# The first transform stage of the later batches: row fold on GpSimd, column fold on VectorE, products in four 64x64 tiles

## The chip, the core and the metric

The kernel runs on one core of one Trainium2 chip. A core has five engines that run their own queues and meet through semaphores: TensorE (PE; its weight loads are shown apart as PEld), VectorE (DVE), ScalarE (ACT), GpSimd (POOL) and SyncE (SP, which here only issues DMAs). The metric is the device time of one execution in microseconds, as the median of several runs. Before the change it is 1962.98 us, the median of three runs (1962.75 to 1963.18).

## What is computed

The reference takes eight batches of 3008 positions by 256 features, all in float32. It applies a Fourier transform along both axes, keeps the real part, and sends it through a two-layer network whose activation is h times cos(h):

```python
X = np.fft.fft(np.fft.fft(x, axis=1), axis=2).real   # x: (8, 3008, 256)
h = X.reshape(24064, 256) @ w_in                     # w_in: (256, 2048)
out = (h * np.cos(h)) @ w_out                        # w_out: (2048, 256)
```

## The kernel before

**The transform.** The 3008 positions are written as 47 rows (s2) by 64 columns (s1). The transform along the positions is therefore done in two stages: first over the 47 rows, for each of the 64 columns, and then over the columns. The input is real, so column i is handled together with column 64 - i: there are 32 pairs, `NI`, numbered i. The transform along the features folds feature d with feature 256 - d, so that 128 numbers are left of each 256, once as a sum (e = 0) and once as a difference (e = 1); the cosines and sines that this needs are multiplied into the network's first weights at the start.

*First stage, in chunks of four pairs (c = 0 to 7).* `load_x` (L151) brings 16 pairs into one of two buffers `xs[p]`, with the 47 rows of column i and the 47 rows of column 64 - i on 110 partitions. `fold` (L237) adds and subtracts features d and 256 - d of a chunk, 110 partitions by 4x127 (508) elements, once for each e; for the first batch VectorE does it, for the later ones GpSimd. `first_half` (L271) then makes two products for each chunk, one for each e, with 110 rows, 64 output columns and 512 moving columns (L286). They write the lower and the upper 64 partitions of one PSUM bank, `pz`. Chunk 0 has its pair 0 apart (L283), and chunks 0 and 4 also compute feature 128 for 16 pairs (`middle`, L253, product at L256). ScalarE copies `pz` to `zs` (L291) with feature 128 beside it (L292), and `store_z` (L298) sends `zs` to DRAM.

*Second stage.* `load_z` reads this back in another order; `second_half` (L321) makes 4 products of 128 columns for each of six groups (L328, bank `pb`), and ScalarE copies them to `pq`. `pz` and `pb` take turns in the one bank with the tag "fft".

**The network.** A batch has six groups of output columns, and a group has eight steps, each with 256 of the 2048 hidden units, so there are 384 steps (48 a batch). Step t has `mm1` (L484: four products into a bank `H`, two with `WC` and two with `WS`), then on ScalarE `act_e` (`ew`, L495), `seed` for the next step's `H` (L454), `act_sin` (L525) and two `act_round` (L515), and on VectorE `dve_h` (L500), `dve_frac` (L519), `dve_g` (L529) and `dve_s` (L540, L550), and at last `mm2` (L574), seven products of 256 columns that are summed over the eight steps in four banks `M`. The second half of the fourth of these banks is not used by `mm2`. The seven products are the fast form of a 2x2 block product: their inputs `S` are sums that VectorE makes. The stages of one step are spread over four turns of the main loop (`LAG` = 3). At the end of a group ScalarE reads the `M` banks (`take_m`, L595), GpSimd adds them up (L626), VectorE transposes (`store_out`, L670) and SP stores.

**What sets the order.** The order is written out by hand in the main loop (L756); every engine runs its queue in that order. The transform of batch b lies beside the network of batch b - 1: `transform` (L364) puts its calls into lists by step number, counted here from the first step of batch b - 1. Calls of `todo` (loads, `first_half`, stores, second half) are issued at the end of a step; calls of `aside` are GpSimd's, and `beside` (L747) ties each of them to the step's last `dve_s` (L550), so that GpSimd starts together with VectorE's reads of PSUM. Before the change a chunk folds in steps o and o + 1, makes its products at the end of step o + 2 and is stored in step o + 3, with o = 7 + 8*(c//2) + 2*(c%2); `load_z` is in step 37, and the six second halves are in steps 41, 43, 45, 49, 52 and 55.

Of the kernel before, what the change touches and what calls it, by code (L numbers as in the profile page):

```python
# [18 lines left out]
ND = 256  # L19
# [16 lines left out]
    return STEP * (r % 16) + 3 * side + r // 16  # L36


def _consts():

    s2 = np.arange(N2)
    j = np.arange(NJ)
    th = 2.0 * np.pi * np.outer(s2, j) / N2
    thm = 2.0 * np.pi * np.outer(46 - s2, j) / N2
    thh = 2.0 * np.pi * np.outer(s2 + 0.5, j) / N2
    z = np.zeros((N2, NJ))
    pad = np.zeros((2 * N2, 16))

    def stack(a, b, c, d):
        m = np.block([[a, b], [c, d]]).reshape(2 * N2, 2, NJ)
        near, far = m[:, :, 0:JA], m[:, :, JA:]
        return np.concatenate(
            [near.reshape(2 * N2, 2 * JA), far.reshape(2 * N2, 2 * (NJ - JA)), pad], axis=1
        )

    LE = stack(np.cos(th), -np.sin(th), np.cos(thm), -np.sin(thm))
    LO = stack(np.sin(th), np.cos(th), -np.sin(thm), -np.cos(thm))
    LE0 = stack(np.cos(th), z, z, np.cos(thh))  # L60
    LO0 = stack(np.sin(th), z, z, np.sin(thh))
    L = np.concatenate([LE, LO, LE0, LO0], axis=1)
    rows = np.zeros((128, 256))
    for side in range(2):
        for r in range(N2):
            rows[_place(side, r)] = L[N2 * side + r]
    L = rows

    k2 = np.arange(64)
    i = np.arange(NI)  # L70
    B = np.zeros((128, NJ, 128))
    for jj in range(NJ):
        phi = 2.0 * np.pi * np.outer(i, 47 * k2 + jj) / SEQ
        blk = np.concatenate([np.cos(phi), np.sin(phi)], axis=0)
        blk[0] = 1.0
        blk[NI] = np.where(k2 % 2 == 0, 1.0, -1.0)
        blk = blk.reshape(2, 2, 16, 64)
        for half in range(2):
            for r in range(2):
                for e in range(2):  # L80
                    p = 64 * half + 32 * e + r
                    B[p : p + 31 : 2, jj, 64 * e : 64 * e + 64] = blk[r, half]

    c = np.arange(ND)
    d = np.arange(128)
    ang = 2.0 * np.pi * np.outer(c, d) / ND
    CS = np.concatenate([np.cos(ang), -np.sin(ang)], axis=1) / TWO_PI
    CS[:, 128] = np.where(c % 2 == 0, 1.0, -1.0) / TWO_PI
    return (
        L.astype(np.float32),  # L90
        B.reshape(128, NJ * 128).astype(np.float32),
        CS.astype(np.float32),
    )
# [28 lines left out]
def kernel(  # L122
# [8 lines left out]
    NB = x.shape[0]  # L131
    L_np, B_np, CS_np = _consts()
    LCS_dr = nc.inline_tensor(
        np.concatenate([L_np, CS_np[0:128], CS_np[128:256]], axis=1), name="dft_L"
    )
    ident_dr = nc.inline_tensor(np.eye(128, dtype=np.float32), name="ident")
    B_dr = nc.inline_tensor(B_np, name="dft_B")

# [9 lines left out]

    xs = [spool.tile([128, XP * ND], FP, tag=f"xp{p}", name="xp") for p in range(2)]

    def load_x(b, p):  # L151
        xv = xs[p][0 : 16 * STEP].rearrange("(e g) c -> e g c", g=STEP)
        i0 = XP * p
        back = nc.sync if b or p else nc.scalar

        def load(queue, g, c0, c1, cols, **more):
            for m in range(3):
                k = 15 if m == 2 else 16
                queue.dma_start(
                    out=xv[0:k, g + m, ND * c0 : ND * c1].rearrange("e (i d) -> e i d", d=ND),  # L160
                    in_=x_r[b, 16 * m : 16 * m + k, cols],
                    **more,
                )

        load(nc.sync, 0, 0, XP, slice(i0, i0 + XP), max_dma_last_dim=2048)
        c0 = 0 if p else 1
        load(back, 3, c0, XP, slice(64 - i0 - c0, 64 - i0 - XP, -1))
        if p == 0:
            load(nc.sync if b else nc.gpsimd, 3, 0, 1, slice(32, 33))

    LCS = cpool.tile([128, 768], FP, tag="LCS", name="LCS")
    L = LCS[:, 0:256]
# [14 lines left out]
    def load_bj(c0, c1):  # L187
        nc.sync.dma_start(out=BJ[:, c0:c1], in_=B_dr.ap()[:, c0:c1])

    def load_ident():  # L190
        nc.sync.dma_start(out=ident, in_=ident_dr.ap())

# [10 lines left out]
    mid = cpool.tile([128, NI], FP, tag="mid", name="mid")  # L203
    nc.sync.dma_start(out=LCS, in_=LCS_dr.ap())
    load_w(0)
    nc.vector.memset(xs[0][0:XR, 0:2048], 0.0)  # L206
    nc.gpsimd.memset(xs[0][0:XR, 2048:4096], 0.0)
    nc.vector.memset(VX[:, 0:512], 1.0)
    nc.vector.memset(ones, 1.0)
    nc.vector.memset(mask, 1.0)  # L210
    nc.vector.memset(mask[0:1], 0.0)
    nc.vector.memset(xs[1][0:XR], 0.0)
    load_x(0, 0)
    for xf in xf0:
        nc.gpsimd.memset(xf[64:128], 0.0)
# [4 lines left out]
    WC = cpool.tile([128, NDFF], FP, tag="WC", name="WC")  # L220
    WS = cpool.tile([128, NDFF], FP, tag="WS", name="WS")
    wn = cpool.tile([128, 16], FP, tag="wn", name="wn")
    nrow = cpool.tile([1, NDFF], FP, tag="nrow", name="nrow")
    xf1 = [cpool.tile([128, 2 * IP * 128], FP, tag=f"xf{i}", name="xf") for i in range(2)]
    for xf in xf1:
        nc.gpsimd.memset(xf[0:XR, 512:1024:128], 0.0)

    bank = {"fft": 1, "M": 4, "H": 3}

# [1 line left out]
        return ppool.tile([128, 512], FP, tag=tag, bufs=bank[tag], name=name)  # L231


    def folded(b, c):
        return (xf1 if b else xf0)[c % 2]

    def fold(b, c, e):  # L237
        lo = IP * (c % 4)
        xv = xs[c // 4].rearrange("r (i d) -> r i d", d=ND)[0:XR, lo : lo + IP]
        fv = folded(b, c).rearrange("r (e i d) -> r e i d", e=2, d=128)[0:XR]  # L240
        if e == 0:
            (nc.scalar.copy if b else nc.gpsimd.tensor_copy)(  # L242
                out=fv[:, 0, :, 0], in_=xv[:, :, 0]
            )
        return (nc.gpsimd if b else nc.vector).tensor_tensor(  # L245
            out=fv[:, e, :, 1:128],
            in0=xv[:, :, 1:128],
            in1=xv[:, :, 255:128:-1],
            op=ALU.subtract if e else ALU.add,
        )  # L250

    def middle(b, p):
        xm = xs[p].rearrange("r (i d) -> r i d", d=ND)[0:XR, :, 128]  # L253
        pm = acc[live[0]][3][64:128, 256 : 256 + XP] if b else psum("pm", "M")[64:128, 0:XP]
        for i0, i1, q in ((0, 1, 2), (1, XP, 0)) if p == 0 else ((0, XP, 0),):
            nc.tensor.matmul(  # L256
                pm[:, i0:i1],
                lhsT=L[0:XR, 64 * q : 64 * q + 64],
                rhs=xm[:, i0:i1],
                start=b == 0,  # L260
                stop=True,
                skip_group_check=b > 0,
            )
        nc.scalar.copy(out=mid[64:128, XP * p : XP * p + XP], in_=pm)

    acc = {}
    started = {}
# [2 lines left out]

    def first_half(b, c):  # L271

        if c % 4 == 0:
            middle(b, c // 4)
        rows = XR if b else 128
        fv = folded(b, c).rearrange("r (e c) -> r e c", e=2)[0:rows]
        LE, LO, LE0, LO0 = (L[0:rows, 64 * q : 64 * q + 64] for q in range(4))
        pz = psum("pz", "fft" if b else "M")
        a = 128 if c == 0 else 0
        for e, (w, w0) in enumerate(((LE, LE0), (LO, LO0))):  # L280
            rows = slice(64 * e, 64 * e + 64)
# [4 lines left out]
            nc.tensor.matmul(  # L286
                pz[rows, a:512], lhsT=w, rhs=fv[:, e, a:512], start=True, stop=True
            )
        tag, n = ("zs", 4) if b or c < 4 else ("pq", 8)
        zs = spool.tile([128, 512], FP, tag=tag, bufs=n, name="zs")  # L290
        nc.scalar.copy(out=zs, in_=pz)  # L291
        nc.scalar.copy(out=zs[64:128, 0:512:128], in_=mid[64:128, IP * c : IP * c + IP])  # L292
# [5 lines left out]
    def store_z(b, c, far):  # L298
# [4 lines left out]
        zd = zds[b, far].rearrange("(h e i r) (j d) -> h i (r j) e d", h=2, e=2, r=2, d=128)  # L303
        zs = zss[b, c].rearrange("(e y) (i d) -> y e i d", e=2, d=128)
        y0 = 2 * JA if far else 0
        for e in range(2):
            queue = nc.scalar if b == 0 and not far and (e or c > 3) else nc.sync
            queue.dma_start(
                out=zd[half, IP * q : IP * q + IP, :, e].rearrange("i y d -> y i d"),
                in_=zs[y0 : y0 + 2 * n, e],  # L310
# [49 lines left out]

    todo = {}
    aside = {}

    def transform(b):  # L364
        t0 = (b - 1) * NG * 8
# [1 line left out]
        def at(o, *call):  # L367
            todo.setdefault(t0 + o, []).append(call)

        at(3, load_x, b, 0)  # L370
        at(14, load_x, b, 1)
        for c in range(NCH):
            o = 7 + 8 * (c // 2) + 2 * (c % 2)
            aside.setdefault(t0 + o, []).append((fold, b, c, 0))
            aside.setdefault(t0 + o + 1, []).append((fold, b, c, 1))
            at(o + 2, first_half, b, c)
            at(o + 3, store_z, b, c, 0)
            at(o + 3, store_z, b, c, 1)
        at(37, load_z, b, 0)
        at(37, load_z, b, 1)  # L380
        for g, o in enumerate((41, 43, 45, 49, 52, 55)):
            at(o, second_half, b, g)

    def fold_weights(e, n, tag="M"):
# [11 lines left out]
        if e:  # L396
            nc.scalar.activation(
                out=W[:, cols], in_=pw, func=AF.Copy, bias=0.0, scale=mask[:, 0:1]
            )
            nc.vector.tensor_copy(out=nrow[:, cols], in_=pw[0:1, :])  # L400
        else:
            nc.scalar.copy(out=W[:, cols], in_=pw)

# [1 line left out]

    def send_wn(n):
        wds[n] = dpool.tile([1, 512], FP, tag="wd", bufs=4, name="wd")
        nc.sync.dma_start(out=wds[n], in_=nrow[:, 512 * n : 512 * n + 512])

    def take_wn(n):  # L410
        nc.sync.dma_start(
# [54 lines left out]
    def seed_first(s):  # L466
        T = s.T
        s.pq, s.nb = ready[s.b, s.grp]
        for u in range(2):
            nc.tensor.matmul(  # L470
                s.H[:, u * T : u * T + T],
                lhsT=nrow[:, 128 * u : 128 * u + 128],
                rhs=s.pq[0:1, T : 2 * T],
                start=False,
                stop=True,
# [249 lines left out]
    for c in range(NCH // 2):  # L725
# [4 lines left out]
    opening = {  # L730
        0: ((combine_w2, 6, 8), (take_wn, 2)) + tuple((store_z, 0, c, 1) for c in (4, 5)),
        1: ((send_wn, 3),) + tuple((store_z, 0, c, 1) for c in (6, 7)) + ((take_wn, 3),),
        2: ((load_z, 0, 1), (load_bj, 1024, NJ * 128)),
        5: ((second_half, 0, 1),),
        10: ((second_half, 0, 2), (load_ident,)),
        14: ((second_half, 0, 3),),
        18: ((second_half, 0, 4),),
        22: ((second_half, 0, 5),),
    }
    per = NG * 8  # L740
    n = len(steps)

    def step(t, last=None):
        s = steps[t] if 0 <= t < n else None
# [11 lines left out]
    for t in range(n + LAG + 1):  # L756
        cur, prev, old, done = step(t), step(t - 1), step(t - 2), step(t - LAG)
        if cur:
            if t % per == 0 and cur.b + 1 < NB:
                transform(cur.b + 1)  # L760
            mm1(cur, 0)
            act_e(cur)
            if t == 0:
# [22 lines left out]
            act_sin(prev)  # L786
        if old:
            dve_s(old, 0)
        if done:
            dve_s(done, 2)  # L790
        ahead = dve_s(old, 1) if old else None
# [50 lines left out]
```

## Time and profile before

| What | Value |
|---|---|
| median of 3 runs | 1962.98 us (1962.75 to 1963.18) |
| the profiled execution, and its span | 1964.43 us, 1962.7 us |
| granted TensorE clock, mean | 0.995 |
| VectorE busy | 1747.2 us (89%) |
| ScalarE busy | 1521.2 us (78%) |
| GpSimd busy | 377.7 us (19%) |
| DMA | 88.67 MB, mean 45 GB/s |

A float32 product shows as two MATMUL records and two LDWEIGHTS records, so 9216 MATMUL records are 4608 products. "Busy" counts overlapping records once. A line of the timeline is the start in us, how long the merged records last, the engine, the line of the kernel, the operation, output<-inputs, the shape and how many records; in square brackets stands the idle time before it and who ended it. L12 is line 12 of the kernel before.

### The profile page before, as it was taken

Reading aid. Unit: us, or ns where it says so; the run is one execution under the profiler, and the core shown is the slowest. Engines: PE = TensorE matmul, PEld = TensorE weight load, DVE = VectorE, ACT = ScalarE, POOL = GpSimd, SP = SyncE. Lnnn points to the kernel's source line nnn. Section 1 sums busy time; section 2 is a strip of 40 time slices with the busy share of each in tenths; the row PEclk is TensorE's granted clock in tenths of the full one; section 3 lists DMA queues with packets and bytes.
Section 4 is the critical chain, followed back from the end, with each engine's and each line's share of the span. In section 5 each row is a group of like instructions: output and inputs, shape, how many; then the busy total and the mean of one; then the engine's idle time right before and its main releaser. Section 6 shows DMA issues by size and latency. Waiting matters only on the chain.

```text
span 1962.7 us, 29008 instructions
## 1 busy us (share of the span) xinstructions
PE 1940.6 (99%) x9216; PEld 1689.6 (86%) x9216; DVE 1747.2 (89%) x3217; ACT 1521.2 (78%) x2762; POOL 377.7 (19%) x432
## 2 busy tenths in 40 slices
PE   7999999999999999999999999999999999999998
PEld 3888899888998889988898888988889888898887
DVE  4888998899889998899889988998899898999998
ACT  2877778777787788777877787778877887778775
POOL 2122202222022211222112221122211222111100
PEclk8999999999999999999999999999999999999999
DMA  6320112202111112120121201211012201110010
GB/s 198 90 67 22 57 25 55 54 22 60 29 50 50 29 54 53 25 57 23 54 54 27 56 24 53 53 50 35 24 49 60 56 22 56 22 28 10 12 23 22
DMA packets 159960, 88.67 MB, mean 45 GB/s; under 512 B 104845, under 2 KB 150204, under 8 KB 158656
## 3 DMA queue, kind: packets, MB, share of 16 engines
q1 hardware_dynamic: 158320, 85.72, 16.7%
q8 instruction: 73, 1.20, 0.3%
q10 hardware_dynamic: 1392, 1.05, 0.2%
q14 instruction: 79, 0.65, 0.1%
q0 software_dynamic: 96, 0.05, 0.0%
HBM read 49.51 MB, written 37.28 MB: 44 GB/s over the span
## 4 chain that ended last, share of the span: by engine, by line
PE 97%; DMA 1%; DVE 1%; ACT 0%; issue 0%; ACTq 0%; POOL 0%; DVEq 0%; POOLq 0%; SPq 0%
PE M L574 58%; PE H L484 34%; PE pz L286 3%; PE pb L328 2%; DMA xp<-in_x_dram 1%; DMA zd<-zs 0%; PE pw L388 0%; DMA z<-zd 0%; PE M L256 0%; DVE r L519 0%; PE pz L283 0%; PE H L470 0%; DVE xp L206 0%; POOL xf L242 0%; DVE ob L670 0%
## 5 line engine op out<-in xcount | busy, mean ns | idle before, releaser
L574 PE MATMUL M<-S,VX 128*128 128x256 f32 (+1 forms) x2304 | 612.8, 375 | 0.0
L574 PEld LDWEIGHTS M<-S,VX 128*128 128x128 f32 x2304 | 438.8, 191 | 48.9
L515 ACT ACTIVATE r<-H 128x512 f32<-128x512 f32 (+1 forms) x384 | 226.0, 589 | 252.9 <-DVE h L500 252.9
L525 ACT ACTIVATE r<-r 128x1024 f32<-128x1024 f32 (+1 forms) x384 | 395.2, 1029 | 24.4 <-DVE r L519 18.2
L500 DVE TENSOR_TENSOR h<-ew,H 128x512 f32<-128x512 f32 (+1 forms) x384 | 259.3, 675 | 165.6 <-PE H L484 90.6
L484 PE MATMUL H<-pq,WC 128*128 128x256 f32 (+1 forms) x1536 | 395.2, 380 | 1.1 <-ACT H L454 1.1
L484 PE MATMUL H<-pq,WS 128*128 128x256 f32 (+1 forms) x1536 | 388.8, 376 | 0.6 <-ACT ew L495 0.5
L574 PE MATMUL M<-r,w 128*128 128x256 f32 (+1 forms) x1536 | 388.0, 375 | 0.0
L454 ACT ACTIVATE H<-nb,wn 128x256 f32<-128x256 f32 (+1 forms) x766 | 362.2, 473 | 13.9
L484 PEld LDWEIGHTS H<-pq,WC 128*128 128x128 f32 x1536 | 284.5, 191 | 73.9 <-ACT r L515 23.5
L574 PEld LDWEIGHTS M<-r,w 128*128 128x128 f32 x1536 | 300.8, 197 | 26.7
L484 PEld LDWEIGHTS H<-pq,WS 128*128 128x128 f32 x1536 | 292.8, 191 | 35.7 <-ACT ew L495 2.0
L495 ACT ACTIVATE ew<-H 128x512 f32<-128x512 f32 (+1 forms) x384 | 225.9, 588 | 73.4 <-PE H L484 68.1
L519 DVE SCALAR_TENSOR_TENSOR r<-r,H 128x512 f32<-128x512 f32 (+1 forms) x384 | 258.8, 674 | 20.4 <-ACT r L515 1.6
L626 POOL TENSOR_TENSOR cb<-cb,mr 128x256 f32<-128x256 f32 (+3 forms) x188 | 157.9, 850 | 541.4 <-DVE S L550 344.5
L540 DVE TENSOR_TENSOR S<-r 128x512 f32<-128x512 f32 (+1 forms) x384 | 259.1, 675 | 0.1
L519 DVE SCALAR_TENSOR_TENSOR r<-r,h 128x512 f32<-128x512 f32 (+1 forms) x384 | 258.6, 673 | 0.0
L529 DVE SCALAR_TENSOR_TENSOR r<-h,r 128x512 f32<-128x512 f32 (+1 forms) x384 | 258.2, 672 | 0.0
L529 DVE SCALAR_TENSOR_TENSOR r<-H,r 128x512 f32<-128x512 f32 (+1 forms) x384 | 256.0, 667 | 0.9 <-ACT r L525 0.5
L515 ACT ACTIVATE r<-h 128x512 f32<-128x512 f32 (+1 forms) x384 | 236.0, 614 | 0.0
L574 PE MATMUL M<-S,w 128*128 128x256 f32 (+1 forms) x768 | 225.7, 375 | 1.0 <-DVE S L550 1.0
L245 POOL TENSOR_TENSOR xf<-xp 110x508 f32<-110x508 f32 x112 | 141.7, 1265 | 436.1 <-DVE S L550 281.6
(75 smaller groups left out, 1449.9 us busy)
## 6 DMA issues: line engine op xcount, KB each, us to landing
out_dram<-ob SPq DMA_DIRECT2D x728, 32.0 KB
xp<-in_x_dram SPq DMA_DIRECT2D x48, 256.0 KB
zd<-zs SPq DMA_DIRECT2D x128, 80.0 KB
z<-zd SPq DMA_DIRECT2D x8, 1280.0 KB
xp<-in_x_dram SPq DMA_DIRECT2D x38, 240.0 KB
nb<-nd SPq DMA_DIRECT2D x40, 128.0 KB
wr<-in_moe_w_in_dram SPq DMA_DIRECT2D x4, 512.0 KB
w<-in_moe_w_out_dram SPq DMA_DIRECT2D x2, 1024.0 KB
```

Of the source, the lines that this page charges most:

```text
L245: return (nc.gpsimd if b else nc.vector).tensor_tensor(out=fv[:, e, :, 1:128], in0=xv[:, :, 1:128], in1=xv[:, :, 255:128:-1], op=ALU.subtr ...
L454: nc.scalar.activation(out=s.H[:, u * T : u * T + T], in_=s.nb[:, 0:T], func=AF.Copy, bias=0.25, scale=wn[:, f : f + 1],)
L484: nc.tensor.matmul(s.H[:, u * T : u * T + T], lhsT=W[:, 128 * f : 128 * f + 128], rhs=s.pq[:, e * T : e * T + T], start=False, stop=True, ...
L495: nc.scalar.mul(out=s.ew[:, 0 : 2 * s.T], in_=s.H[:, 0 : 2 * s.T], mul=2.0)
L500: nc.vector.tensor_tensor(out=s.h[:, 0 : 2 * T].rearrange("p (u t) -> p u t", u=2)[:, :, ::-1], in0=s.ew[:, 0 : 2 * T].rearrange("p (u t) ...
L515: nc.scalar.activation(out=r, in_=h, func=AF.Copy, bias=BIG, scale=1.0)
L519: nc.vector.scalar_tensor_tensor(out=r, in0=r, scalar=-BIG, in1=h, op0=ALU.add, op1=ALU.subtract)
L525: nc.scalar.activation(out=r, in_=r, func=AF.Sin, bias=0.0, scale=SIN_SCALE)
L529: nc.vector.scalar_tensor_tensor(out=r, in0=h, scalar=-0.25, in1=r, op0=ALU.add, op1=ALU.mult)
L540: return nc.vector.tensor_tensor(out=sv[:, 0:2], in0=gv[:, 2:3].to_broadcast([128, 2, T]), in1=gv[:, 0:4:3], op=ALU.subtract,)
L574: nc.tensor.matmul(acc[key][m // 2][:, 256 * (m % 2) : 256 * (m % 2) + T], lhsT=w, rhs=a, start=first, stop=s.fp == 7, skip_group_check=True,)
L626: return nc.gpsimd.tensor_tensor(out=o, in0=a, in1=b, op=ALU.subtract if less else ALU.add)
```

## The change

Only batches 1 to 7 are changed; batch 0 keeps its way. Three things are different.

- **The row fold comes first.** `load_later_x` puts the two columns of a pair on the same partitions (row s of one beside row S - s of the other), 16 of the 32 pairs on partitions 0 to 48 and the other 16 on 64 to 112 ("sets"). A load is made in four calls of seven DMAs, and the two unpaired columns (0 and 32) have four DMAs of their own (`load_ends`). GpSimd's call in `aside` is now `fold_rows`: 113 partitions by 512 elements, once for each e, in place of the fold over features. VectorE has a new list, `between`, issued in the middle of a step: `fold_cols`, which folds the features of what GpSimd left, 113 by 2x127 (254) elements, and once a batch the unpaired columns, 113 by 127. ScalarE copies feature 0.
- **The products are 64x64 tiles.** A chunk has four products (`first_half_later`): for each e and each set, with 49 rows, 64 output columns and 256 moving columns. Set 0 writes `pz`, set 1 writes the unused half of the fourth `M` bank, which ScalarE sets to zero a step earlier (`clear_spare`). ScalarE copies two pieces of 128x256 in place of one of 128x512. Feature 128 takes four products of 7 or 8 columns for 16 pairs (`middle_later`); with chunk 0 there are a fifth one of 1 column and two of 128 columns for the unpaired columns.
- **The order moves.** Batches 2 to 7 load x in steps -20 to -17 and -9 to -6, that is 28 and 39 steps into the network of batch b - 2; batch 1 loads in steps 2 to 5 and 13 to 16. The products of odd chunks, and their stores, come one step later; `load_z` is in step 38, and the first three second halves in 42, 44 and 46. A chunk is stored by eight DMAs in place of four.

```diff
+    def load_later_x(b, p, s, set_):
+        i0 = 16 * set_ + 8 * p
+        skip = 1 if s and i0 == 0 else 0
+        cols = slice(64 - i0 - skip, 56 - i0, -1) if s else slice(i0, i0 + 8)
+        to = xs[p].rearrange("r (s i d) -> r s i d", s=2, d=ND)[:, s, skip:8]
+        for k in range(7):
...
+            nc.sync.dma_start(out=to[part], in_=x_r[b, rows, cols])
...
+    def clear_later():
+        nc.gpsimd.memset(xz, 0.0)
+        for xf in xf1:
+            nc.gpsimd.memset(xf[:, 256:512:128], 0.0)
+        nc.gpsimd.memset(xfz[:, 128:129], 0.0)
...
+    def fold_rows(b, c, e):
+        lo = 2 * (c % 4) * ND
+        xv = xs[c // 4].rearrange("r (s c) -> r s c", s=2)[0:XL, :, lo : lo + 2 * ND]
+        return nc.gpsimd.tensor_tensor(
+            out=xs2[e][0:XL],
+            in0=xv[:, 0],
+            in1=xv[:, 1],
+            op=ALU.subtract if e else ALU.add,
+        )
+
+    def fold_cols(to, src, e):
+        fv = to.rearrange("r (e i d) -> r e i d", e=2, d=128)[0:XL, e]
+        xv = src.rearrange("r (i d) -> r i d", d=ND)[0:XL]
+        nc.vector.tensor_tensor(
+            out=fv[:, :, 1:128],
+            in0=xv[:, :, 1:128],
+            in1=xv[:, :, 255:128:-1],
+            op=ALU.subtract if e else ALU.add,
+        )
+        if e == 0:
+            nc.scalar.copy(out=fv[:, :, 0], in_=xv[:, :, 0])
...
+    def middle_later(pz, p):
+        pm = pz[64:128, 256:272]
+        for set_ in range(2):
+            i0 = 1 if set_ == p == 0 else 0
+            for s in range(2):
+                xm = xs[p].rearrange("r (s i d) -> r s i d", s=2, d=ND)[0:XL, s, i0:8, 128]
+                nc.tensor.matmul(
+                    pm[:, 8 * set_ + i0 : 8 * set_ + 8],
+                    lhsT=weights(2 + set_, 0, XL),
+                    rhs=xm,
+                    start=s == 0,
+                    stop=s == 1,
+                )
+        if p == 0:
+            nc.tensor.matmul(
+                pm[:, 0:1], lhsT=weights(4, 0, XL), rhs=xz[0:XL, 128:129], start=True, stop=True
+            )
...
+    def clear_spare():
+        nc.scalar.activation(
+            out=acc[live[0]][3][:, 256:512],
+            in_=VX[:, 0:256],
+            func=AF.Copy,
+            bias=0.0,
+            scale=0.0,
+        )
+
+    def first_half_later(b, c):
+        pz = psum("pz")
+        spare = acc[live[0]][3][:, 256:512]
+        if c % 4 == 0:
+            middle_later(pz, c // 4)
+        if c == 0:
+            for e in range(2):
+                nc.tensor.matmul(
+                    pz[64 * e : 64 * e + 64, 0:128],
+                    lhsT=weights(4 + e, 0, XL),
+                    rhs=xfz[0:XL, 128 * e : 128 * e + 128],
+                    start=True,
+                    stop=True,
+                )
+        xf = xf1[c % 2]
+        for e in range(2):
+            for set_ in range(2):
+                r0, r1 = 64 * set_, 64 * set_ + XT
+                c0 = 128 if set_ == c == 0 else 0
+                nc.tensor.matmul(
+                    (spare if set_ else pz)[64 * e : 64 * e + 64, c0:256],
+                    lhsT=weights(e, r0, r1),
+                    rhs=xf[r0:r1, 256 * e + c0 : 256 * e + 256],
+                    start=set_ == 0,
+                    stop=True,
+                    skip_group_check=set_ == 1,
+                )
+        zs = spool.tile([128, 512], FP, tag="zs", bufs=4, name="zs")
+        nc.scalar.copy(out=zs[:, 256:512], in_=spare)
+        nc.scalar.copy(out=zs[:, 0:256], in_=pz[:, 0:256])
...
+        zss[b, c] = zs
...
+        if b:
+            for e in range(2):
+                for h in range(2):
+                    nc.sync.dma_start(
+                        out=zd[h, 2 * c : 2 * c + 2, :, e].rearrange("i y d -> y i d"),
+                        in_=zs[y0 : y0 + 2 * n, e, 2 * h : 2 * h + 2],
+                    )
+            return
...
-        at(3, load_x, b, 0)
-        at(14, load_x, b, 1)
+        for p, o in enumerate((2, 13) if b == 1 else (-20, -9)):
+            for k in range(4):
+                at(o + k, load_later_x, b, p, k % 2, k // 2)
+        at(4 if b == 1 else -16, load_ends, b)
         for c in range(NCH):
             o = 7 + 8 * (c // 2) + 2 * (c % 2)
-            aside.setdefault(t0 + o, []).append((fold, b, c, 0))
-            aside.setdefault(t0 + o + 1, []).append((fold, b, c, 1))
-            at(o + 2, first_half, b, c)
-            at(o + 3, store_z, b, c, 0)
-            at(o + 3, store_z, b, c, 1)
-        at(37, load_z, b, 0)
-        at(37, load_z, b, 1)
-        for g, o in enumerate((41, 43, 45, 49, 52, 55)):
+            f = o + 2 + c % 2
+            for e in range(2):
+                aside.setdefault(t0 + o + e, []).append((fold_rows, b, c, e))
+                between.setdefault(t0 + o + e + 1, []).append(
+                    (fold_cols, xf1[c % 2], xs2[e], e)
+                )
+            at(f - 1, clear_spare)
+            at(f, first_half, b, c)
+            at(f + 1, store_z, b, c, 0)
+            at(f + 1, store_z, b, c, 1)
+        for e in range(2):
+            between.setdefault(t0 + 7 + e, []).append((fold_cols, xfz, xz, e))
+        at(38, load_z, b, 0)
+        at(38, load_z, b, 1)
+        for g, o in enumerate((42, 44, 46, 49, 52, 55)):
             at(o, second_half, b, g)
...
         if old:
             dve_s(old, 0)
+        for call in between.pop(t, ()):
+            call[0](*call[1:])
         if done:
             dve_s(done, 2)
```

Left out above: the constants of the tiles (`V`), `load_ends`, the clearing of the new buffers in step 2 (`clear_later` is called there, and `V` is loaded there), the start's memsets on all 128 partitions, and the row of weights `nrow`, which moves into four short-lived buffers.

## The prediction, made before the changed kernel ran

> **What bounds the kernel.** The page's busy times come first, then the chain that ended last, then the table of engines by stretch.
>
> ```profile
> PE 1940.6 (99%) x9216; PEld 1689.6 (86%) x9216; DVE 1747.2 (89%) x3217; ACT 1521.2 (78%) x2762; POOL 377.7 (19%) x432
> ...
> PE 97%; DMA 1%; DVE 1%; ACT 0%; issue 0%; ACTq 0%; POOL 0%; DVEq 0%; POOLq 0%; SPq 0%
> ```
>
> ```profile
> 300.00:540.00 240.00, 240.00 (x1154) 210.59 (x1153) 216.26 (x399) 190.54 (x348) 48.97 (x54) 1.00 0.17 45
> ```
>
> In a batch's stretch PE is busy 240.00 of 240.00 us at full clock; all else is hidden. A gain must shorten PE's queue without making PE wait, so I look at what PE does around a chunk (timeline, PE alone):
>
> ```profile
> 341.45 0.59 PE L574 MATMUL M<-S,w 128*128 128x256 f32 x2
> 341.97 1.08 PE L286 MATMUL pz<-xf,LCS 110*64 110x512 f32 x4
> 342.98 1.13 PE L484 MATMUL H<-pq,WC 128*128 128x256 f32 x4
> 343.95 1.03 PE L574 MATMUL M<-r,w 128*128 128x256 f32 x4
> ...
> 347.40 0.59 PE L574 MATMUL M<-S,w 128*128 128x256 f32 x2
> 347.83 1.03 PE L484 MATMUL H<-pq,WC 128*128 128x256 f32 x4
> 348.70 0.59 PE L574 MATMUL M<-r,w 128*128 128x256 f32 x2
> ```
>
> Without a chunk it is 1.30 us from `M<-S,w` to `M<-r,w`, with one 2.50 (1.21 by unrounded starts): a chunk costs PE **1.21 us**. All 42 chunks without feature 128 cost within 1 ns of that, those with c = 4 1.32 and those with c = 0 1.44, so PE never waits for a chunk. The pieces, from single records: 0.096 to enter (beyond the 0.213 that a record of 256 columns takes), 0.480 from the first record of a product to its second, 0.006 between the two products, 0.521 from there to the next weight load, and 0.105 in which that load isn't hidden. A record of 512 columns takes 0.427, so 0.053 of the 0.480 and 0.094 of the 0.521 are fill and drain. The two products run together: within 20 ns of 341.97 the timeline starts both.
>
> ```profile
> 341.97 0.65 PE L286 MATMUL pz<-xf,LCS 110*64 110x512 f32 x2
> ```
>
> **PE's terms.** *Tiles.* Four products of 256 columns replace two of 512. If all four tiles run together, a chunk costs 0.096 + (0.213 + 0.053) + 3 x 0.006 + (0.213 + 0.094) + 0.105 = 0.79 us, 0.42 less; over 56 chunks 23.5 us. If only the two column halves run together, as now, two rounds of 256 columns take what one of 512 takes: 1.20. No record of before has tiles on different rows; the ends are 0.79 and 1.20. I take 0.79: the nearest row, two tiles on different columns, overlaps fully, and here both the rows and the PSUM banks of the two sets differ. The Trainium skill has only this beside it: "TensorE: Matmul & The Clock Gate", section "Measured speedup vs the span model", gives 10.6 times for 16 small tiles; by it all four overlap, and no run here shows it yet.
>
> *Feature 128.* It now takes four products of 7 or 8 columns at c = 4, a fifth at c = 0, on one column tile, with 113 rows, hence in another tile shape than the four that follow. The nearest records:
>
> ```profile
> 331.39 0.22 PE L256 MATMUL M<-xp,LCS 110*64 110x1 f32 x1
> 331.41 0.32 PE L283 MATMUL pz<-xf,LCS 110*64 110x128 f32 x1
> 331.47 0.27 PE L256 MATMUL M<-xp,LCS 110*64 110x1 f32 x2
> 331.57 0.27 PE L283 MATMUL pz<-xf,LCS 110*64 110x128 f32 x1
> 331.59 0.21 PE L256 MATMUL M<-xp,LCS 110*64 110x15 f32 x1
> ```
>
> Such records follow each other by 0.06 us (0.08 after the first). At c = 4 that is 8 x 0.06 + 0.02 = 0.50, and one more change of shape at about 0.1: a chunk of 1.40, 0.08 more than now. At c = 0 it is 10 records (0.62), two of 128 columns behind them on that tile (0.21), the other parity hidden on the other tile, and again 0.1 and some records' gaps: 1.78, 0.34 more than now. Counted from 0.79, the extras over seven batches are 7 x 0.60 + 7 x 0.98 = 11.1, against 7 x 0.11 + 7 x 0.23 = 2.4 now: 8.7 us. They also wait for up to eight DMA semaphores; those loads land dozens of steps before (batch 1's one step), so I add nothing, at most 0.3 us each at 14 places.
>
> Tiles and feature 128 make 23.5 - 8.7 = **14.8 us less on PE**.
>
> **What the other engines must hide.** *VectorE* gets 112 folds of 113x254 and 14 of 113x127. Nearest is the sum of 128x256 from SBUF (L550), 419 ns long; two in a row start 0.335 apart, which is what a fold delays the queue:
>
> ```profile
> 369.80 0.42 DVE L550 TENSOR_TENSOR S<-r,S 128x256 f32<-128x256 f32 x1
> 370.14 0.42 DVE L550 TENSOR_TENSOR S<-S,r 128x256 f32<-128x256 f32 x1
> 370.55 0.69 DVE L500 TENSOR_TENSOR h<-ew,H 128x512 f32<-128x512 f32 x1
> ```
>
> The ends are 0.335 and 0.42. A fold waits for GpSimd, which ran 3 us earlier. Behind the fold in the queue is the sum that `M<-S,w` of the same step needs. That product starts at 371.14 and its weight load 0.21 earlier; the sum ends at 370.22. With the folds of this and the previous step it ends at 370.89: it fits by 0.04. The steps before hold the transposes (L670), so this is the tightest place.
>
> *ScalarE* gets a clear (0.47, as L454) and two copies of 128x256 (392 ns each, as L595) for one of 586 ns: +0.67 us a chunk, 37 us of its 440 idle. Behind the copies is `ew`, for which PE waits. I follow an even chunk: `h` comes 0.6 late (two folds), so the roundings and the copies end late, `ew` by 0.5, and in the next step, which also reads two M banks, the rounding ends 0.8 after VectorE wants it. VectorE's sum of the step after is then late for PE by 0.14, and the clear makes the following `ew` late by 0.1. So PE stops for some 0.25 us. This holds for the two groups of a batch whose even chunk (2, 6) has no feature 128; chunks 0 and 4 give 0.6 to 1.0 us of time. 14 x 0.25 = **3.5 us back**.
>
> *GpSimd* folds 113x512 in place of 110x508: the adds of 128x512 (1273 ns) stand beside 1265 ns, tied to the same `dve_s`. No cost. *SP and DMA:* x goes from 15 DMAs a batch to 60, the stores of z from 32 to 64. At 0.8 us a load (four at 363.21 in 3.34) four steps of seven loads take 22 us of 19, beside stores: SP falls up to 15 us behind from step 28 on. Behind it wait output stores (their buffer is wanted 8 steps later), stores of z (16 steps) and nothing due sooner; by step 37 it has caught up. `load_z` is now behind step 38's output stores, some 4 us, with four steps until its product as before. Batch 1's last loads stand behind step 5's round trip to DRAM and may hold one fold for 1 to 2 us. The start's memsets are as wide as before: nothing.
>
> **Sum.** -14.8 + 3.5 = -11.3 us on the profiled execution: 1964.4 - 11.3 = 1953.1. The median of the runs is 1.45 under that execution, so I forecast **1951.7 us**; with stalls of 0 to 9 us its own range is 1947 to 1960.
>
> **Rivals.**
> - *The row halves run in turn* (the other side). A chunk then costs 1.20, and feature 128 adds its 8.7 us unpaid. Gain 56 x 0.01, hence +8.1: **1971**. It decides at the tiles' overlap: below 8.7 of 23.5 us, some 40%, the change loses. For it: no record shows row tiles. Against it: the column tiles' 6 ns.
> - *The records keep the program's order.* Then each tile's second record holds up the next tile's first: starts at 0, 0.27, 0.27, 0.49, 0.49, 0.70, 0.71, 0.92, so a chunk costs 1.43 us, 0.22 more than now: 56 x 0.22 + 8.7 = +21, **1984**. "TensorE: Matmul & The Clock Gate" of the Trainium skill states this rule under "The mechanism": MATMULs start and end in program order. This trace disagrees: the product of L283 starts at 331.41, ahead of the second product of L256 (331.53), which precedes it in the program.
> - *The squeeze takes the gain.* With folds at 0.42 and ScalarE's copies at their full length (0.98 us a chunk for 0.78, and 0.2 for their semaphores), PE stops by up to 0.55 in all 28 groups: 15 us back, **1963**. For it: VectorE's margin of 0.04; against: each later step has 0.6 to 1.1 more.
> - *It doesn't do what it says* (loads or PSUM waits keep the tiles apart): as the first rival.
>
> **Chances.** Forecast 0.62 (1951.7), squeeze 0.13 (1960 to 1966), row halves in turn 0.15, program order 0.06, the rest 0.04. The range must take in the squeeze and most of the row halves: 1947 to 1972. A measurement of this kernel tells 0.2%, 3.9 us, from no change. Faster: the forecast and a little of the squeeze, 0.66; the same 0.10; slower 0.24.
>
> **What would show it.** Of the timeline: the chunk's records start four together within 30 ns, and from `M<-S,w` to `M<-r,w` it is 2.1 us, not 2.5. PEld's waits for VectorE's `S` and ScalarE's `ew` come to some 3.5 us in all. VectorE is near 1790 us busy, ScalarE near 1558, GpSimd unchanged. I am wrong if the records start in pairs, if PE's idle before `S`, `ew` or x loads passes 10 us, or if a fold takes longer than 0.42 us because GpSimd reads beside it.

## The result, and the profile after

| Kernel | Median, us | Runs | Profiled execution, and its span |
|---|---|---|---|
| before, in the same job | 1962.82 (1959.01 to 1964.42) | 12 | 1964.43, 1962.7 (an earlier run) |
| changed | 1967.51 (1961.98 to 1969.86) | 12 | 1966.13, 1964.4 |

The ratio is 1.0023, with a 95% interval of 1.0013 to 1.0033: 4.7 us slower, where 11.3 us faster was forecast. The page of the changed kernel, busy times and the chain that ended last:

```profile
PE 1926.7 (98%) x9524; PEld 1690.4 (86%) x9524; DVE 1782.5 (91%) x3343; ACT 1531.3 (78%) x2881; POOL 379.6 (19%) x434
...
PE 84%; DVE 7%; issue 3%; DMA 2%; ACT 2%; SPq 1%; DVEq 0%; ACTq 0%; POOL 0%; POOLq 0%
```

PE is 13.9 us less busy, near the 14.8 forecast, and yet the span is 1.7 us longer: PE now waits. The chain tells the same: PE's share fell from 97% to 84%, and other engines, issue and DMA stand in it. In a stretch of the table of engines (start and end, length, then PE, PEld, DVE, ACT, POOL busy, then the granted clock, DMA's share and GB/s) PE has 1.53 us idle, where before it had none:

```profile
300.00:540.00 240.00, 238.47 (x1199) 211.17 (x1199) 220.63 (x416) 192.50 (x366) 49.17 (x54) 1.00 0.17 43
```

**The tiles work.** PE's timeline around a chunk without feature 128, with the records that start it:

```profile
350.46 0.59 PE L730 MATMUL M<-S,w 128*128 128x256 f32 x2
350.99 0.43 PE L385 MATMUL pz<-xf,V 49*64 49x256 f32 x1
350.99 0.43 PE L385 MATMUL M<-xf,V 49*64 49x256 f32 x1
351.00 0.43 PE L385 MATMUL pz<-xf,V 49*64 49x256 f32 x1
351.00 0.43 PE L385 MATMUL M<-xf,V 49*64 49x256 f32 x1
351.25 0.38 PE L385 MATMUL pz<-xf,V 49*64 49x256 f32 x1
...
352.55 1.03 PE L730 MATMUL M<-r,w 128*128 128x256 f32 x4
```

All four start within 20 ns, and from `M<-S,w` to `M<-r,w` it is 2.09 us. By unrounded starts, and against the 1.295 us of a step without a chunk, each of the 42 chunks costs 0.790 us; the forecast had 0.79. "TensorE: Matmul & The Clock Gate" of the Trainium skill, section "Measured speedup vs the span model", lets many small tiles overlap, and this trace now agrees for four.

**Feature 128 does not.** The same timeline at a chunk with c = 4:

```profile
652.94 0.59 PE L730 MATMUL M<-S,w 128*128 128x256 f32 x2
653.47 0.67 PE L341 MATMUL pz<-xp,V 113*64 113x8 f32 x8
655.01 0.43 PE L385 MATMUL pz<-xf,V 49*64 49x256 f32 x1 [0.87 <-ACT mid L352]
...
655.60 1.13 PE L640 MATMUL H<-pq,WC 128*128 128x256 f32 x4
```

Between the small products and the tiles PE stands idle for 0.87 us: the first tile waits for `mid`, ScalarE's copy of what the small products wrote. ScalarE's timeline shows why that copy is late:

```profile
653.65 0.60 ACT L671 ACTIVATE r<-H 128x512 f32<-128x512 f32 x1 [0.99 <-DVE h L656]
654.14 0.62 ACT L671 ACTIVATE r<-h 128x512 f32<-128x512 f32 x1
654.79 0.17 ACT L352 COPY mid<-pz 64x16 f32<-64x16 f32 x1
```

The copy takes 0.17 us, but it stands behind the step's two roundings. A chunk with c = 4 costs 2.21 to 2.41 us (median 2.33) for a forecast of 1.40, one with c = 0, behind the opening, 2.53 to 2.64 (median 2.53) for 1.78. The table of waits (total us, times, longest) has both places:

```profile
PE pz L385 <- ACT mid L352: 6.3, 7, 1.0
...
PE pz L373 <- ACT mid L352: 4.7, 7, 0.9
```

In 55 chunks (the first lies in the opening) PE spends 68.5 us before and 64.8 after; the forecast's sizes give 53.7.

**The opening loses 5 us.** I compare the start of VectorE's `h` of each step with before. In the changed kernel steps 1 to 6 are 1.33 us early (such offsets differ between executions), step 8 is 3.78 us late, step 10, behind the first chunk, 4.78. SP's queue before, and after:

```profile
57.71 9.46 SPq L159 DMA_DIRECT2D xp<-in_x_dram  x9
72.60 0.26 SPq L350 DMA_DIRECT2D nd<-pq  x1
73.71 0.34 SPq L351 DMA_DIRECT2D nb<-nd  x1
```

```profile
56.94 16.47 SPq L178 DMA_DIRECT2D xp<-in_x_dram  x21
73.52 2.63 SPq L183 DMA_DIRECT2D xz<-in_x_dram  x4
76.25 0.22 SPq L495 DMA_DIRECT2D nd<-pq  x1
77.35 0.36 SPq L496 DMA_DIRECT2D nb<-nd  x1
77.77 2.40 SPq L178 DMA_DIRECT2D xp<-in_x_dram  x7
```

Step 5's round trip (row 0 of `pq` to DRAM and back to all partitions) stands behind 25 loads and comes 3.6 us later. ScalarE's seed of step 8 needs it:

```profile
80.65 0.99 ACT L610 ACTIVATE H<-nb,wn 128x256 f32<-128x256 f32 x2 [4.50 <-DMA nb<-nd]
```

### The profile page after: what moved, and what is told of

The parts are those of the page before. It is cut to its first block, busy times and chain, and to the rows that moved or that the text cites. A ratio compares the mean times of both kernels' runs of the same rounds, so it can differ in the third digit from the quotient of the medians.

```text
span 1964.4 us, 30495 instructions
## 1 busy us (share of the span) xinstructions
PE 1926.7 (98%) x9524; PEld 1690.4 (86%) x9524; DVE 1782.5 (91%) x3343; ACT 1531.3 (78%) x2881; POOL 379.6 (19%) x434
## 3 DMA queue, kind: packets, MB, share of 16 engines
q10 hardware_dynamic: 1392, 1.05, 0.2%
## 4 chain that ended last, share of the span: by engine, by line
PE 84%; DVE 7%; issue 3%; DMA 2%; ACT 2%; SPq 1%; DVEq 0%; ACTq 0%; POOL 0%; POOLq 0%
PE M L730 50%; PE H L640 30%; PE pb L473 2%; PE pz L385 2%; DVE r L685 1%; ACT r L671 1%; DVE S L696 1%; DVE h L656 1%; DMA xp<-in_x_dram 1%; DVE r L675 1%; DVE S L706 1%; DVE ob L826 1%; DMA zd<-zs 1%; DMA out_dram<-ob 1%; SPq L836 1%
## 5 line engine op out<-in xcount | busy, mean ns | idle before, releaser
L640 PEld LDWEIGHTS H<-pq,WC 128*128 128x128 f32 x1536 | 283.3, 190 | 54.9 <-issue 11.1
L300 POOL TENSOR_TENSOR xs<-xp 113x512 f32<-113x512 f32 x112 | 143.0, 1277 | 460.5 <-DVE S L706 403.7
```

Source lines behind the costliest of these rows:

```text
L300: return nc.gpsimd.tensor_tensor(out=xs2[e][0:XL], in0=xv[:, 0], in1=xv[:, 1], op=ALU.subtract if e else ALU.add,)
L640: nc.tensor.matmul(s.H[:, u * T : u * T + T], lhsT=W[:, 128 * f : 128 * f + 128], rhs=s.pq[:, e * T : e * T + T], start=False, stop=True, ...
```

## The experiments

Theory A: the time lies in these two places, the wait for the copy (about 11.8 us: 0.93 and 0.75 us over forecast, seven times each) and SP's queue in the opening (5 us). Theory B, the rival: something spread over all chunks takes it, such as the squeeze of VectorE and ScalarE. Each kernel ran in jobs beside the kernel before; ratios are to that.

| Kernel | Median, us | Ratio, 95% interval |
|---|---|---|
| E1 feature 128 behind the tiles | 1952.59 | 0.9948 (0.9935 to 0.996) |
| E1 again | 1955.39 | 0.9955 (0.9943 to 0.9968) |
| E2 batch 1's first loads split | 1965.43 | 1.0009 (1.0 to 1.0018) |
| E3 both | 1951.81 | 0.9944 (0.9931 to 0.9956) |
| E3 again | 1953.57 | 0.9948 (0.9936 to 0.9961) |
| E4 both, GpSimd's loads tied | 1948.7 | 0.9923 (0.9911 to 0.9936) |
| E4 again | 1950.32 | 0.993 (0.9917 to 0.9942) |
| E5 as E1, round trip from GpSimd | 1951.71 | 0.9939 (0.9927 to 0.9952) |
| E6 before, 24 loads for 9 | 1970.02 | 1.003 (1.0018 to 1.0042) |
| E7 as E3, clear twice | 1955.59 | 0.9961 (0.9947 to 0.9975) |
| E8 as E4, loads two steps earlier | 1950.0 | 0.9928 (0.9915 to 0.9942) |
| E10 only the copy behind the tiles | 1953.16 | 0.9945 (0.9932 to 0.9959) |

### E1: feature 128 behind the tiles

```diff
-        if c % 4 == 0:
-            middle_later(pz, c // 4)
         if c == 0:
...
+        if c % 4 == 0:
+            middle_later(pz, c // 4)
         zs = spool.tile([128, 512], FP, tag="zs", bufs=4, name="zs")
```

> The products of feature 128 are issued behind the chunk's four tiles instead of ahead of them; nothing else differs from the changed kernel. Theory A: in the changed kernel the tiles of chunks 0 and 4 wait until ScalarE has copied feature 128 out of the same PSUM bank, 0.9 us each, 14 times. Then a chunk 4 takes PE 1.40 us instead of 2.33 and a chunk 0 1.78 instead of 2.53, 11.8 us in all: 1967.5 becomes about 1956. Rival B: the 0.9 us are the second change of tile shape and the many semaphores of those products; they stay wherever the products stand, chunks 0 and 4 keep 2.3 and 2.5 us, and the time stays at 1967 to 1968.

Measured: 1952.59, 14.9 us less than the changed kernel and below the 1956 expected, so theory A. PE's timeline at a chunk with c = 4:

```profile
648.12 0.38 PE L383 MATMUL pz<-xf,V 49*64 49x256 f32 x1
648.43 0.63 PE L341 MATMUL pz<-xp,V 113*64 113x8 f32 x8
648.99 1.13 PE L640 MATMUL H<-pq,WC 128*128 128x256 f32 x4
```

No wait is left; the copy is made while PE goes on with `H`. A chunk with c = 4 costs 1.35 us, with c = 0 1.83, without feature 128 0.790 as in the changed kernel. From step 14 to step 336, over 13 of the 14 places, `h` gains 14.4 us on the kernel before; in the changed kernel it gains 3.3. The difference, 11.1 us, is the wait, and the first place (step 9 to 10) adds 1.0. The rest of the 14.9 is not shown to be this edit's; the opening still loses 5.0 us.

### E10: only the copy behind the tiles

`middle_later` keeps its products and its place; its copy becomes a call of its own.

```diff
+    def copy_middle(pz, p):
+        pm = pz[64:128, 256:272]
         nc.scalar.copy(
...
+        if c % 4 == 0:
+            copy_middle(pz, c // 4)
         zs = spool.tile([128, 512], FP, tag="zs", bufs=4, name="zs")
```

> The changed kernel, in which the products of feature 128 stay ahead of the four tiles and only ScalarE's copy of them is called behind the tiles. Theory (PE's 0.9 us at a chunk with feature 128 are the wait for that copy, which reads the bank that the tiles write, and not the small products' place or shape): no wait of the tiles for ScalarE, a chunk with c = 4 costs about 1.4 us, the opening as in the changed kernel, so about as E1 in its two jobs, 1952.6 to 1955.4. Rival (going from 113 rows to 49 rows and from one column tile to four costs the time, whatever is copied): 2.3 us for a chunk with c = 4 still, 1967.

Measured: 1953.16 us, and in PE's timeline the tiles follow the small products at once:

```profile
649.40 0.59 PE L735 MATMUL M<-S,w 128*128 128x256 f32 x2
649.93 0.63 PE L341 MATMUL pz<-xp,V 113*64 113x8 f32 x8
650.49 0.43 PE L388 MATMUL pz<-xf,V 49*64 49x256 f32 x1
```

A chunk with c = 4 costs 1.352 us and one with c = 0 1.735, so neither the place of the small products nor the change of tile shape costs more than forecast. It is the copy, called between products that write the same bank. "PSUM — Partial Sum Buffer" of the Trainium skill, section "PSUM bank collisions raise a hardware error", asks for a semaphore between engines that touch one bank in the same 32 partitions, whatever the columns, and calls a guard by whole banks the simple version. The trace agrees: the copy reads columns 256 to 271, the tiles write 0 to 255, and in the changed kernel they wait for it, 0.87 us in the profile of a chunk with c = 4. Before, `middle` wrote an `M` bank and the chunk's products `pz`: no wait.

### E2 and E3: batch 1's first loads split

```diff
-            nc.sync.dma_start(out=to[part], in_=x_r[b, rows, cols])
+            queue.dma_start(out=to[part], in_=x_r[b, rows, cols])
# queue: nc.gpsimd for batch 1, first buffer, set 1, and for its load_ends; else nc.sync
```

> Batch 1's first loads: set 1 and the unpaired columns (18 of the 32 DMAs) go through GpSimd's queue, the rest stay on SyncE's. Theory A: the 5 us that PE loses between steps 7 and 8 come from SyncE's queue, where 25 loads of 0.8 us stand ahead of the row that step 8's seed needs, and 7 more ahead of the first fold. Then those 5 us go, and the runs also spread less: about 1962.5. Rival B: the transfers themselves are late (as many small packets behind the same weights), so the queue does not matter: 1967 to 1968, the first fold again waits until about 84 us.

> Both edits together. Theory A on both counts: 11.8 and 5 us less than the changed kernel, about 1951, which is what was forecast for the change; PE is then idle less than 4 us between 100 and 1740 us. If the squeeze of VectorE and ScalarE was only hidden by the waits at chunks 0 and 4, it shows here as idle time of PE before S or ew, up to 0.25 us in each of 28 groups, and the time is nearer 1956.

Measured: E2 is 2.1 us under the changed kernel, where 5 were expected. E3 is near the 1951 expected, but only because E1 alone had come out below its 1956; it is 0.8 under E1. The stall itself is gone: E3's `nd` is issued at 74.24 and `nb` at 75.42, and step 8 is as late as step 6 to 0.14 us in both. But all steps start later, 2.84 us after those of before in E2 and 1.65 in E3. E2's profile loses another 2.7 us from step 9 to step 10, and its granted clock is 0.57 from 95 to 99 us; the changed kernel loses 0.8 us there, with the clock at 1.00. GpSimd's and PE's timelines of E3 show a new collision:

```profile
26.75 3.45 POOL L179 DMA_DIRECT2D xp<-in_x_dram  x7
30.19 0.54 POOL L184 DMA_DIRECT2D xz<-in_x_dram  x1
32.02 1.58 POOL L184 DMA_DIRECT2D xz<-in_x_dram  x3 [1.29 <-DMA xp<-in_x_dram]
33.71 4.03 POOL L179 DMA_DIRECT2D xp<-in_x_dram  x7
```

```profile
37.64 2.08 PE L474 MATMUL pb<-BJ,z 128*128 128x128 f32 x8 [4.17 <-DMA z<-zd]
```

GpSimd's queue is empty there and its loads wait for nothing but one another, so they are issued some 30 us ahead of the steps that call them, beside the first read of z (at 34.44), for which PE waits 4.17 us; in E1 it was 1.97. That this collision is the cause is so far an argument.

### E4: the same, with GpSimd's loads tied

```diff
+            if b == 1 and p == 0 and set_ and s == k == 0:
+                beside(ins, tie[0])      # tie[0]: dve_s(old, 1) of turn 2
```

> As E3, but the first of GpSimd's 18 loads of batch 1 waits for VectorE's last sum of step 0, so that they can't start at 27.7 us, where E3 issued them beside the first read of z. Theory (in E3 these loads collide with that read: PE waited 4.17 us for z there and 1.97 in E1, and all later steps came some 4 us later): the wait for z is 2 us again, the steps start as in E1, and no seed waits for nb at step 8; E1's 4.7 us are saved whole: 1952 - 4 = 1948 us. Rival (executions start a few us apart by chance): 1952, as E3.

> The kernel of E3 again. Theory (GpSimd's untied loads delay the first read of z): PE waits over 3 us for z, the first steps come later than in E1 and E4, and the time is 1951 to 1952, some 3 us above E4. Rival (chance): the first steps as early as in E1, and the time that of E4.

> The kernel of E4 again. Theory: PE waits for z 1 to 2 us, the first steps as in E1, 1948.7, some 4 us under E1. Rival (chance): 1951 to 1952, as E3.

> The kernel of E1 again, beside E3, E4 and E8 on one chip. If executions' starts differ by chance alone, its first steps may lie on either side of those of before; 1952.6.

Measured: E4 1948.7, and on one chip E4 1950.32, E3 1953.57, E1 1955.39. E4 and E8 (below) are the fastest versions, E4 at 0.9923 and 0.993 of the kernel before. PE waits for z 1.01 and 1.89 us in the two profiles of E4, 4.17 and 4.66 in those of E3. "DMA: Bandwidth & Descriptors" of the Trainium skill, section "Issuing engines are not separate DMA queues", says that DMAs issued by ScalarE, SyncE or GpSimd run on the same 16 engines and interleave. The trace agrees: in E3 the other issuing engine let `nd` go out 2.0 us earlier than in the changed kernel (74.24 for 76.25), but PE's wait for z grew from 1.97 us in E1 to 4.17.

The offsets of `h` against before, by kernel, show how much differs between executions:

| Kernel | Step 6, us | Wait for z, us | Lost from step 6 to 8, us |
|---|---|---|---|
| changed | -1.33 | 2.13 | 5.1 |
| E1, again | -2.59, 0.56 | 1.97, 2.18 | 5.0, 5.5 |
| E10 | -0.74 | 2.08 | 5.5 |
| E2 (untied) | 2.84 | 5.02 | 0.1 |
| E3 (untied), again | 1.65, 3.60 | 4.17, 4.66 | 0.1, 0.2 |
| E7 (untied) | 0.58 | 2.55 | 0.1 |
| E4 (tied), again | -2.08, -1.52 | 1.01, 1.89 | 2.2, 1.9 |

The changed kernel, E1 and E10 are the same program up to here and spread over 3.2 us, so one profile proves little. The granted clock is part of it: from 30 to 55 us it is 0.86 in E1 and 0.73 in E1 again, whose steps 6 lie 3.2 us apart. It is 0.73 in E2 and in both profiles of E3, and 0.86 and 0.80 in those of E4, so the table can't tell how much of E3's delay is the wait for z and how much the clock, and whether the longer wait lowers the clock stays open. For the tie speak the times on one chip: all five runs of E4 (1948.65 to 1951.30) lie under all five of E3 (1951.89 to 1956.17).

E4 does not get the whole 5 us: its seed still waits 2.72 us.

```profile
70.93 0.23 SPq L499 DMA_DIRECT2D nd<-pq  x1
74.81 0.36 SPq L500 DMA_DIRECT2D nb<-nd  x1
```

`nd` is early, but `nb` follows 3.9 us later, not 1.1.

### E8: E4 with the loads called two steps earlier

```diff
-        for p, o in enumerate((2, 13) if b == 1 else (-20, -9)):
+        for p, o in enumerate((0, 13) if b == 1 else (-20, -9)):
...
-        at(4 if b == 1 else -16, load_ends, b)
+        at(2 if b == 1 else -16, load_ends, b)
```

> As E4, but batch 1's first 32 loads are called two steps earlier (SP's 14 in steps 0 and 1, ahead of the second read of z; GpSimd's 18 still wait for VectorE's last sum of step 0). Theory (what is left of the opening's stall in E4, 2.2 us between steps 7 and 8, is the round trip of nd and nb behind SP's loads: nd was issued at 70.9, nb at 74.8, 3.9 us later, where before it was 1.1): nd finds the queue empty, the seed of step 8 does not wait, 2 us less than E4: 1946.5. Rival (the later read of z, or the nrow transfers that now stand among loads, hold up steps 1 to 6 by as much): 1948.7 or more.

Measured: 1950.0 beside E4's 1950.32, no gain, and 2.5 us are still lost from step 6 to step 8. SP has issued all its loads by 58 us, and the round trip is longer yet:

```profile
58.01 0.35 SPq L466 DMA_DIRECT2D z<-zd  x1
58.41 0.43 SPq L228 DMA_DIRECT2D BJ<-dft_B  x1
59.06 0.32 SPq L231 DMA_DIRECT2D V<-dft_V  x1
70.51 0.25 SPq L499 DMA_DIRECT2D nd<-pq  x1
75.41 0.33 SPq L500 DMA_DIRECT2D nb<-nd  x1
```

My theory of E4's remainder falls: it isn't the issue of loads ahead on SP. The transfers are another matter. In the table of engines by stretch DMA is 0.41 busy from 72 to 74.4 us and 0.00 in the microsecond behind it, and the trace's DMA records show packets of both queues until then, SP's of 1536 bytes, the width of `V`, until 73.9 and `nd`'s own 1 KB at 74.31. Which of them held it, GpSimd's loads or the reads now moved behind SP's, was not tried and stays open.

### E5: only the round trip moved

The line for `nb` is changed in the same way.

```diff
+        queue = nc.gpsimd if (b, g) == (0, 1) else nc.sync
-        nc.sync.dma_start(out=nd[:, 0:T], in_=pq[0:1, T : 2 * T])
+        queue.dma_start(out=nd[:, 0:T], in_=pq[0:1, T : 2 * T])
...
```

> As E1, all loads on SP, but the two DMAs of step 5's round trip (nd, nb) are issued by GpSimd, so that they don't stand behind the 25 loads. Theory: the seed of step 8 finds nb in time, and what is left of the 4.7 us is the row fold of step 7, which waits for the last load until 83.2 us in place of 80, and holds VectorE's column fold behind it: 1 to 3 us, so 1949 to 1951. Rival A (the round trip is not what the seed waits for, or it takes as long from GpSimd): 1952.6 as E1. Rival B (the fold alone gives the whole stall): 1952.6 too, but with the seed in time and VectorE waiting at the fold.

Measured: 1951.71, 0.9 under E1 with overlapping intervals, above the range that I expected. In its trace 3.2 us are lost from step 6 to step 8, for 5.0 and 5.5 in E1: the seed waits 1.41 us, and the row fold, at 85.60, waits for the last load.

```profile
80.05 0.99 ACT L611 ACTIVATE H<-nb,wn 128x256 f32<-128x256 f32 x2 [1.41 <-DMA nb<-nd]
...
85.60 1.26 POOL L300 TENSOR_TENSOR xs<-xp 113x512 f32<-113x512 f32 x1 [8.58 <-DMA xp<-in_x_dram]
```

So the round trip and the late fold are two stalls, one behind the other, and moving one uncovers the other.

### E6: the kernel before with more loads

```diff
+            n = (6 if g else 4) if (b, p) == (1, 0) and c1 > c0 + 1 else 16
...
+                for r in range(0, 15 if m == 2 else 16, n):
```

> The kernel before, in which only batch 1's first 9 loads are cut into 24 (same bytes and places, pieces of 4 or 6 rows in place of 16). Theory (the number of issues on SP ahead of the round trip is what costs 5 us in the opening): 24 issues of some 0.7 to 0.8 us end at about 76 us in place of 67, nd is issued there and not at 72.6, the seed of step 8 waits for nb some 4 us, and the time is 1963.3 + 4 to 5 = 1967 to 1968. Rival (the stall has to do with the new folds): 1963.3, no change.

Measured: 6.2 us slower than the kernel before, 1 to 2 more than expected. SP's and ScalarE's timelines:

```profile
56.42 20.51 SPq L161 DMA_DIRECT2D xp<-in_x_dram  x24
77.03 0.35 SPq L352 DMA_DIRECT2D nd<-pq  x1
78.26 0.34 SPq L353 DMA_DIRECT2D nb<-nd  x1
```

```profile
81.24 0.99 ACT L456 ACTIVATE H<-nb,wn 128x256 f32<-128x256 f32 x2 [5.05 <-DMA nb<-nd]
```

Nothing but the count of loads was changed, the bytes and places are the same, and the stall of the changed kernel is there: 5.2 us between steps 6 and 8, and no microsecond more in the 320 steps behind (the offset stays at 3.9). So more issues on SP ahead of the round trip are enough for this stall, without the new folds.

### E7: the clear twice

```diff
             at(f - 1, clear_spare)
+            at(f - 1, clear_spare)
```

> E3 with ScalarE's clear of the spare bank half issued twice for each of the 56 chunks, 0.38 us (some 0.27 in the queue) more each time. Theory (ScalarE has slack in a batch, and the squeeze of 3.5 us forecast for it is not there): 1952 to 1954. Rival (ScalarE is near its limit, and the forecast's ew comes late by what is added less 0.1 to 0.2): in 28 to 56 places 0.1 to 0.3 us, so 1955 to 1968, with PE waiting for ew or S.

Measured: 1955.59, at the low edge of what the rival gives. Its interval overlaps that of E3; the traces are clearer. From step 14 to step 336 E3 gains 14.45 us on before and E7 10.74, so 3.7 us for 54 more clears. The wait that grows is that of PE's weight loads for `ew`, in E7:

```profile
PEld H L642 <- ACT ew L653: 9.4, 32, 1.4
```

In E3 it is 1.8 us at 2 places. So ScalarE has room for the clear that the change adds, and not for another: the squeeze is real, one operation further on than I put it.

## Why the prediction was wrong, point by point

- **Tiles: right.** 0.79 forecast, 0.790 measured. Both rivals about them fall: row halves don't run in turn, and the records don't keep the program's order; each tile's second record came 0.26 us behind its first, with the other tiles' first records in between, against the rule of "TensorE: Matmul & The Clock Gate" of the Trainium skill, section "The mechanism".
- **Feature 128: wrong, the step that failed first.** I priced its products (1.40 and 1.78; 1.35 and 1.74 to 1.83 without the wait) and wrote that they "also wait for up to eight DMA semaphores", to which I added nothing. I didn't ask who reads their result and what stands behind that reader: the copy is in the program between the small products and the tiles, in the bank that the tiles write. That is 11.8 us, more than the whole forecast gain.
- **PE's sum: right without the wait.** 14.8 us were forecast for 56 chunks; in 55 of them PE spends 14.9 us less in E1 than before.
- **SP: wrong.** I wrote "Batch 1's last loads stand behind step 5's round trip to DRAM and may hold one fold for 1 to 2 us". I looked at the 7 loads behind it and not at the 25 ahead of it, though 0.8 us an issue, the figure that I used, puts `nd` at 57 + 25 x 0.8 = 77 us; it came at 76.25. This cost 5.1 us.
- **VectorE: right.** It is busy for 1782.5 us (1790 forecast), a fold takes 417 ns, and PE waits for `S` at two places, 2.3 us in all.
- **ScalarE: the term was mis-sized.** I gave 3.5 us back; in steady state nothing is, for in E1 PE is busy 1590.00 of the 1590.00 us from 110 to 1700. The clear takes 380 ns for 470, the copies 368 and 382 for 392, and they start 0.27 apart. ScalarE is busy for 1531.3 us, not 1558. E7 shows how near the edge is.
- **GpSimd: right.** A row fold takes 1277 ns for 1273, and it is busy for 379.6 us.
- **The sum.** The forecast of 1951.7 and the result lie 15.8 us apart: 11.8 + 5.1 - 3.5 = 13.4. The other 2.4 lie within the spread of executions; the two profiled executions themselves, 1953.1 forecast and 1966.13 measured, lie 13.0 apart. The changed kernel's twelve runs spread over 8 us, along with the granted clock: the two at a mean of 0.998 took 1962.0 and 1962.1, those at 0.992 and 0.993 1967.7 to 1969.9.
- **The range held by luck.** 1967.51 lies within the stated 1947 to 1972, but the range was drawn wide for the squeeze and for row halves in turn, and neither is what happened.

My sign of being wrong, "PE's idle before `S`, `ew` or x loads passes 10 us", named the wrong waits. The one that passed 10 us was for ScalarE's copy.

## What to carry to other kernels

Cost a moved operation by its reader too: list what each result is read by, whether the read stands between two writes of the same PSUM bank, and what is queued ahead of the reader on its engine; a copy of 0.17 us cost PE 0.7 us (c = 0) or 0.9 us (c = 4) at each of 14 places. When a transfer is cut into more issues, look for every small round trip that is queued behind them. And a load moved to an empty queue starts at once, not where the program calls it: tie it to a point in time, or it can collide with what was there.

## What was not expected of the hardware

- SP's issues have no fixed price: in the changed kernel 21 loads in a row take 0.78 us each, the seven behind `nb` 0.34 each; in E6 pieces of a quarter of the rows or a little more took 0.85 each, and the nine whole ones before 1.05.
- The round trip of `nd` (1 KB) takes from its issue to that of `nb` 1.1 us where nothing else is under way, 3.7 to 4.9 where loads from two queues are (E4, E8).
- Four 64x64 tiles cost PE 0.790 us for 1.21 of the two halves. With c = 4 the place of the small products costs nothing, 1.352 us behind the tiles (E1) and ahead of them (E10); with c = 0 it is 1.83 behind and 1.74 ahead.
